# First pair's queries turned in two column parts, 24 zero products, one conversion step fewer at the first mixing, row factors and last scaling rearranged

## The chip, the cores and the metric

The kernel runs on one core of a Trainium2 chip. The time is the device time of one execution in microseconds (us), the median of several runs. The engines are TensorE (PE, with its weight loads as PEld), VectorE (DVE), ScalarE (ACT), GpSimd (POOL) and SyncE (SP, which only issues transfers here). Each works through its own queue in program order.

## The reference

Three layers follow one another on float32 data, batch B = 4, sequence S = 576. First an attention with rotated queries and keys over 8 heads of 64:

```python
q_rot, k_rot = (rotate(q), rotate(k))
scores = scale * np.matmul(q_rot, k_rot.transpose(0, 1, 3, 2))
scores = scores - np.max(scores, axis=-1, keepdims=True)
attn = np.exp(scores)
attn = attn / (np.sum(attn, axis=-1, keepdims=True) + 1e-09)
return np.matmul(attn, v).astype(np.float32)
```

`rotate` multiplies with cosine and sine tables and adds. Its result, laid out as (B, S, 512), goes through a gated layer: `h = gelu(x @ w_in)` split into u and v, v normalized over its row, mixed over the sequence, and

```python
v_s = np.einsum('ts,bsd->btd', w_sg, v_n) + b_sg[None, :, None]
gated = u * v_s
return (x + gated @ w_out).astype(np.float32)
```

Last come 4 experts, each a causal attention with one head of 64. Every row takes the two experts with the largest logits, weighted by a softmax over the two; the expert's output is `a @ v @ wo[e]`, scaled by that weight and by the softmax's row sum, and added to `out`.

## The kernel before, in words

Numbers that need float32 precision are held as two parts, a high one rounded to the fp32r type and a low one (the value less the high part). A product of two such numbers takes the three products high-high, high-low, low-high on TensorE. `split` makes the parts: ScalarE copies the high one, POOL (or VectorE) subtracts.

**Stage one, the attention** (lines 333 to 695), works on 16 pairs of heads (`Work`). A pair has nine row blocks x = 0 to 8. `slot(k)`, called with k = 9 n + x, writes the instructions of all engines by hand in this order: the exponentials of block x (ScalarE, `exps`), the scores of block x + 1 (TensorE, `scores`, into one of two PSUM buffers), the transposes of block x - 1 (TensorE, `turn`), the row maximum of block x + 1 (VectorE, `maxima`), the copies of the transposed block (`place`, ScalarE or VectorE), and in some slots parts of the product with the values (`av`). The engine wrapper keeps every instruction in program order (`fixed[0] = True`). So the scores of a block wait until the exponentials two blocks earlier have freed their buffer.

The tile `t` of a pair holds its queries or keys and, beside them, the same with the halves of each head exchanged. Turning is two products with the tables `rp` and an addition (`rope`, steps 0, 1 and 2). For all pairs but the first, POOL does the turning, `parts` makes the high and low part, and transfers issued by SP (`fill_k`, `fill_q`) copy these into the layouts that the scores read: `q2` (high part of one head above low part of the other), `qz` (high part with zeros beside it), `kh`. `fill_q` gets a tuple `part`; pair 1 calls it with both parts at once, later pairs with (0,) and (1,) apart.

The first pair goes another way, since nothing can hide its preparation: `first` (line 386) turns k and then q on VectorE, and ScalarE, VectorE and POOL write the layouts themselves, with no transfers. Meanwhile TensorE multiplies a tile of zeros (`warmed(40)`, line 658; each product takes two passes). Then come the loads of pairs 1 and 2, POOL's two products for each of pair 1's tiles (lines 663 and 667), and the first scores and maximum. The additions of pair 1 follow on VectorE in slots 2 and 3:

```python
if n == 0 and x in (2, 3):
    works[1].rope(3 - x, (2,), DVE)
```

In slots 0 to 3 TensorE gets two more zero products each.

**Stage two, the gated layer** (lines 729 to 975). `unit(g, *side)` writes TensorE's work of one block, then interleaves the steps of the two blocks before it with side work: `(lu, 3)` means three steps of the generator that converts `w_out` from its raw form (`load_split64`, lines 213 to 247; its VectorE steps are a maximum, a shift, and two combinations through PSUM). `mixed` (line 857) is the mixing over the sequence: 28 passes, then on VectorE a scale-and-add in PSUM and a product with u, then a split. It uses one of three PSUM buffers `S`. Line 938 is the first batch's mixing:

```python
for dc in range(4):
    unit(mixed(0, dc), (lu, (3, 3, 4, 4)[dc]))
```

**Stage three, the experts** (lines 978 to 1468), has 8 pairs of experts (`Causal`, two for each batch) in `slot3`, again nine blocks each. `factor` makes the row factors of a pair: the sums plus a small number (ScalarE), the reciprocal (VectorE), and four small products with the expert's weight on POOL. TensorE transposes them, and a small transfer out and three in spread them (`spread_factor`); `finish` multiplies the result with them and splits it into `zh` and `zl`, on POOL with a few exceptions. `Output.product` multiplies these with `wo` in three passes for each half of the inner dimension, and `Output.store` copies a block to SBUF and sends it out. For the very last pair the factors are spread by TensorE instead (`spread_here`), and lines 1446 to 1467 write the end by hand: transposes and values of the last block, `product` of block 3, spread, store of 3, `finish`, product and store of block 4, then of blocks 0 and 1.

## Time and profile before

| | |
|---|---|
| median of three runs | 675.15 us (675.15, 675.15, 676.3) |
| profiled execution, its own time | 674.28 us |
| its span, first to last instruction | 672.5 us |
| granted TensorE clock, mean | 1.00 |
| busy: PE, DVE, ACT, POOL | 662.9, 446.6, 433.6, 342.3 us |

The times of single instructions come from the one profiled execution; its own time is what sums of them are measured against. A matmul's end is modelled by the profiler, and a TensorE that is shown busy may still work on zeros.

In rows of the timeline the columns are: start in us, duration in us, engine, source line (L59 is the helper through which all instructions go), operation, what it writes and reads, shapes, number of instructions merged, and in brackets the idle time of the engine before it with what ended it. SPq is the transfer queue of SyncE.

### The profile page before, as it was taken

What the parts mean: (1) busy time and instruction counts of PE and PEld (TensorE: products, weight loads), DVE (VectorE), ACT (ScalarE), POOL (GpSimd) and SP (SyncE); (2) the same over time, 40 slices, a digit from 0 to 9 for tenths busy, and PEclk for the clock granted to TensorE, in tenths of its full rate; (3) what the DMA queues carried; (4) which work ended last, traced back from release to release, by engine and by line L of the source; (5) the groups of instructions that cost most, each with busy time, mean ns of one, the idle gap of its engine ahead of it and who ended that gap; (6) DMA issues with size and microseconds to landing.
All of it is one profiled execution on the core that took longest, in us unless ns stands there. A gap on an engine that the chain in (4) does not pass through costs nothing.

```text
span 672.5 us, 13535 instructions
## 1 busy us (share of the span) xinstructions
PE 662.9 (99%) x4741; PEld 585.5 (87%) x4741; DVE 446.6 (66%) x1011; ACT 433.6 (64%) x1033; POOL 342.3 (51%) x333
## 2 busy tenths in 40 slices
PE   8999999999999999999999999999999999999997
PEld 8777777777777777798999999999999999999885
DVE  5877777767777776578964764664247666656674
ACT  6777777877878777673563473472146776666774
POOL 2877788888888832642456127206212451542320
PEclk9999999999999999999999999999999999999999
DMA  7798888887888852661374243055466364553522
GB/s 270 209 283 269 249 237 248 242 239 241 228 254 227 249 150 90 182 189 34 118 222 143 89 134 115 12 142 161 121 182 150 92 171 96 135 160 76 143 82 79
DMA packets 64449, 112.83 MB, mean 168 GB/s; under 512 B 18991, under 2 KB 24190, under 8 KB 64382
## 3 DMA queue, kind: packets, MB, share of 16 engines
q1 hardware_dynamic: 61646, 106.29, 54.8%
q10 hardware_dynamic: 2736, 5.68, 2.8%
q8 instruction: 38, 0.62, 0.4%
q14 instruction: 29, 0.24, 0.1%
HBM read 58.06 MB, written 18.98 MB: 115 GB/s over the span
## 4 chain that ended last, share of the span: by engine, by line
PE 87%; DVE 4%; DMA 3%; ACT 2%; issue 1%; POOL 1%; SPq 1%; POOLq 0%; ACTq 0%; DVEq 0%
PE ps_S L59 46%; PE ps_o L59 16%; PE ps_t L59 13%; PE ps_f L59 5%; PE ps_l L59 3%; PE ps_s L59 3%; DMA ws<-in_w_sg_dram 1%; DMA mask<-in_cst_dram 1%; DVE ga L59 1%; DMA q<-lo 0%; DVE nmax L59 0%; DVE t L59 0%; DMA r<-d 0%; DMA sr<-rd 0%; ACT vh L59 0%
## 5 line engine op out<-in xcount | busy, mean ns | idle before, releaser
L59 DVE TENSOR_REDUCE nmax<-ps_S 128x1 f32<-128x576 f32 x144 | 108.8, 756 | 54.3 <-PE ps_S L59 51.6
L59 ACT ACTIVATE e<-ps_S,nmax 128x576 f32<-128x576 f32 x144 | 107.9, 749 | 34.2 <-DVE nmax L59 32.6
L59 PE MATMUL ps_t<-ident,e 128*128 128x128 f32 x776 | 118.1, 273 | 0.0
L59 PEld LDWEIGHTS ps_t<-ident,e 128*128 128x128 f32 x776 | 94.2, 140 | 3.7 <-ACT wih L59 0.4
L59 PE MATMUL ps_S<-kh,q 128*128 128x288 f32 x352 | 84.9, 333 | 2.6 <-ACT e L59 1.4
L59 POOL TENSOR_TENSOR t<-t,rp 128x576 f32<-128x576 f32 x60 | 84.6, 1431 | 0.1
L59 PEld LDWEIGHTS ps_S<-kh,q 128*128 128x128 f32 x352 | 52.2, 189 | 28.8 <-issue 12.8
L59 PE MATMUL ps_o<-g,v 128*64 128x320 f32 (+1 forms) x512 | 72.7, 415 | 0.0
L59 ACT COPY g<-ps_t 128x512 f32<-128x512 f32 x95 | 55.6, 586 | 23.3 <-PE ps_t L59 23.2
L59 POOL TENSOR_TENSOR lo<-t,hi 128x576 fp32r<-128x576 f32 x30 | 43.1, 1438 | 43.6 <-DVE hi L59 42.2
L59 PE MATMUL ps_S<-lo,q 128*128 128x288 f32 x304 | 65.2, 295 | 0.0
L59 PEld LDWEIGHTS ps_o<-g,v 128*64 128x64 f32 x512 | 32.4, 136 | 24.3 <-issue 4.9
L59 PE MATMUL ps_S<-yh,w 128*128 128x288 f32 x256 | 51.8, 304 | 0.0
L59 POOL TENSOR_TENSOR yl<-x,yh 128x640 fp32r<-128x640 f32 (+1 forms) x16 | 25.0, 1564 | 51.6 <-ACT yh L59 51.5
L59 ACT ACTIVATE e<-e,nmax 128x128 f32<-128x128 f32 (+4 forms) x72 | 42.3, 588 | 13.6 <-DVE nmax L59 13.5
L59 PEld LDWEIGHTS ps_S<-lo,q 128*128 128x128 f32 x304 | 48.6, 188 | 0.0
L59 POOL TENSOR_TENSOR t<-t 128x576 f32<-128x576 f32 x28 | 39.7, 1418 | 2.2
L59 ACT ACTIVATE ga<-ga 128x512 f32<-128x512 f32 (+1 forms) x34 | 22.3, 656 | 26.9 <-DVE ga L59 26.9
L59 PEld LDWEIGHTS ps_S<-yh,w 128*128 128x128 f32 x256 | 38.7, 189 | 0.1
L59 POOL TENSOR_TENSOR xl<-sa,xh 128x576 fp32r<-128x576 f32 x12 | 17.7, 1484 | 40.9 <-ACT xh L59 34.7
L59 DVE CUSTOM_DVE_ANT_0 e<-ps_s,mask 128x128 f32<-128x128 f32 (+3 forms) x64 | 31.0, 486 | 7.9 <-PE ps_s L59 6.0
L59 POOL TENSOR_TENSOR gxl<-u,gxh 128x576 fp32r<-128x576 f32 x16 | 22.8, 1429 | 25.3 <-ACT gxh L59 25.3
(283 smaller groups left out, 1758.5 us busy)
## 6 DMA issues: line engine op xcount, KB each, us to landing
t<-in_qk_dram SPq DMA_DIRECT2D x32, 576.0 KB
kh<-hi SPq DMA_DIRECT2D x92, 144.0 KB
q<-hi SPq DMA_DIRECT2D x30, 288.0 KB
q<-lo SPq DMA_DIRECT2D x38, 144.0 KB
v<-in_v_dram SPq DMA_DIRECT2D x16, 320.0 KB
sa<-xr SPq DMA_DIRECT2D x16, 288.0 KB
xd<-sa SPq DMA_DIRECT2D x16, 288.0 KB
xr<-xd SPq DMA_DIRECT2D x16, 288.0 KB
```

The lines of the kernel that those rows point to most:

```text
L59: ins = op(*a, **k)
```

## The change

The diff has five parts.

1. `first` becomes a generator in steps. It turns k whole and the first 320 columns of q, then writes the layouts for these columns (with VectorE making the low parts), and only in slots 0 to 2 turns and lays out the remaining 256 columns (their low parts on POOL). Pair 1's q products on POOL move from ahead of the first scores into slot 1, behind those low parts; its q addition on VectorE moves from slot 3 to slot 4. The zero products at the start are 24 in place of 40.
2. `fill_q` orders the copies by part: for a call with both parts, the two of the high part come first, then the two of the low part.
3. The first mixing takes 1, 3, 4 and 5 conversion steps in place of 3, 3, 4 and 4.
4. In the slots of the third pair of the experts' stage (n = 2), the four small products for the factors of the pair before it go to VectorE. The other pairs' stay on POOL.
5. At the end, the spread stands behind the first of block 3's three last passes, and the two others and block 4's come after it. The scaling and splitting of the last 256 columns go in two halves of 128, and all four stores come at the end. Block 1's store uses another SBUF buffer.

```diff
--- before.py
+++ after.py
@@ -167,7 +167,7 @@
 
                 todo = [twice(a, q2[a, 0, 0:S], qz[a, 0], qh[a, :]), (q2[c, 0, 0:S], ql[a, :]),
                         twice(c, q2[c, 1, 64:640], qz[c, 1], qh[c, :]), (q2[a, 1, 64:640], ql[c, :])]
-                todo = [x for i, x in enumerate(todo) if i % 2 in part]
+                todo = [x for h in part for x in todo[h::2]]
             else:
                 todo += [(q2[c, 1, 0:512], qh[c, 0:512]), (qz[c, 1, 64:S], qh[c, 0:512]), (q2[a, 1, 0:512], ql[c, 0:512])]
             if not self.turned:
@@ -393,27 +393,40 @@
                 def low(o, x, h, engine=DVE):
                     engine.tensor_tensor(o, x, f(h), op=ALU.subtract)
 
-                for t in (k, q):
+                def turn(t, s):
                     for i in range(2):
-                        DVE.tensor_tensor(t[:, i], t[:, i], rp[:, i], op=ALU.mult)
-                    DVE.tensor_tensor(t[:, 0], t[:, 0], t[:, 1], op=ALU.add)
-                q, k, s, s1 = q[:, 0], k[:, 0], slice(0, S), slice(64, 640)
+                        DVE.tensor_tensor(t[:, i, s], t[:, i, s], rp[:, i, s], op=ALU.mult)
+                    DVE.tensor_tensor(t[:, 0, s], t[:, 0, s], t[:, 1, s], op=ALU.add)
+
+                u, w = slice(0, 320), slice(320, S)
+                turn(k, slice(0, S))
+                turn(q, u)
+                yield
+                t, q, k = q, q[:, 0], k[:, 0]
                 ACT.copy(kh[a, 0], k[a])
                 ACT.copy(kh[c, 0], k[a])
+                ACT.copy(q2[a, 0, u], q[a, u])
+                ACT.copy(qz[a, 0, u], q[a, u])
                 ACT.copy(kh[c, 1], k[c])
+                ACT.copy(kh[a, 1], k[c])
+                ACT.copy(qz[c, 1, u], q[c, u])
                 hi = one.tile([P, S], F32R, tag="hi1", name="hi1")
                 DVE.tensor_copy(hi, k)
                 low(kl, k, hi)
-                ACT.copy(kh[a, 1], k[c])
-                ACT.copy(q2[a, 0, s], q[a])
-                ACT.copy(qz[a, 0], q[a])
-                ACT.copy(qz[c, 1], q[c])
-                u, w = slice(0, 256), slice(256, S)
                 low(q2[c, 0, u], q[a, u], q2[a, 0, u])
-                DVE.tensor_copy(q2[c, 1, s1], q[c])
-                low(q2[a, 1, 64:320], q[c, u], q2[c, 1, 64:320])
-                low(q2[a, 1, 320:640], q[c, w], q2[c, 1, 320:640], POOL)
+                DVE.tensor_copy(q2[c, 1, 64:384], q[c, u])
+                low(q2[a, 1, 64:384], q[c, u], q2[c, 1, 64:384])
+                yield
+                turn(t, w)
+                yield
+                ACT.copy(q2[a, 0, w], q[a, w])
+                ACT.copy(qz[a, 0, w], q[a, w])
                 low(q2[c, 0, w], q[a, w], q2[a, 0, w], POOL)
+                DVE.tensor_copy(q2[c, 1, 384:640], q[c, w])
+                low(q2[a, 1, 384:640], q[c, w], q2[c, 1, 384:640], POOL)
+                yield
+                ACT.copy(qz[c, 1, w], q[c, w])
+                yield
 
             def rope(self, x, steps=(0, 1, 2), engine=POOL):
                 t = self.ts[x]
@@ -544,6 +557,10 @@
 
             if w:
                 w.exps(x)
+            if k in (1, 2):
+                next(first)
+            if k == 1:
+                works[1].rope(0, (0, 1))
             if x == 0 and p:
                 p.out(False)
             if x == 4 and p:
@@ -572,8 +589,8 @@
             if x == 0 and p:
                 p.factor(0)
 
-            if n == 0 and x in (2, 3):
-                works[1].rope(3 - x, (2,), DVE)
+            if n == 0 and x in (2, 4):
+                works[1].rope(int(x == 2), (2,), DVE)
             if wk and not (nx and x == 5):
                 if late:
                     wk.place(4)
@@ -655,16 +672,17 @@
                 PE.matmul(warm[:, 0:P], zero, zero, start=True, stop=True)
 
         fixed[0] = True
-        warmed(40)
+        warmed(24)
         works[0].load(0)
         works[0].load_values()
-        works[0].first()
+        first = works[0].first()
+        next(first)
+        next(first)
         works[1].load(1)
         works[1].rope(1, (0, 1))
         works[1].load_values()
         works[2] = Work()
         works[2].load(2)
-        works[1].rope(0, (0, 1))
         works[0].start()
         works[0].scores(0)
         works[0].maxima(0)
@@ -673,6 +691,8 @@
         for k in range(9 * B * NP + 7):
             n, x = divmod(k, 9)
             slot(k)
+            if k == 0:
+                next(first)
             if k < 4:
                 warmed(2)
             if x in W_AT[4 if n == NP * B - 1 else min(n, 2 + n % 2)]:
@@ -936,7 +956,7 @@
             unit(values(1, tb), then=ln, n=1)
         run(ln)
         for dc in range(4):
-            unit(mixed(0, dc), (lu, (3, 3, 4, 4)[dc]))
+            unit(mixed(0, dc), (lu, (1, 3, 4, 5)[dc]))
         for b in range(1, B):
             at = attended(bx, b + 1) if b + 1 < B else iter(())
             for tb in range(0 if b > 1 else 2, NKB - b % 2):
@@ -1076,10 +1096,10 @@
             def rows(self, tb):
                 return slice(P * tb, P * tb + (P if tb < 4 else 64))
 
-            def product(self, tb, t, c):
+            def product(self, tb, t, c, part=slice(0, 3)):
                 sl = self.rows(tb)
                 zh, zl = self.z
-                for pi, (l, r) in enumerate(((zh, wo_[0]), (zh, wo_[1]), (zl, wo_[0]))):
+                for pi, (l, r) in list(enumerate(((zh, wo_[0]), (zh, wo_[1]), (zl, wo_[0]))))[part]:
                     PE.matmul(t[0:sl.stop - sl.start, :], l[:, c, sl], r[:, c],
                               start=(c == 0 and pi == 0), stop=(c == 1 and pi == 2))
 
@@ -1087,7 +1107,9 @@
                 sl, b = self.rows(tb), self.b
                 m = sl.stop - sl.start
                 act = b < B - 1 or tb in (1, 3, 4)
-                if act:
+                if b == B - 1 and tb == 1:
+                    o = wk.tile([P, S], F32, tag="r", name="ob", bufs=1)[:, 0:DM]
+                elif act:
                     o = wk.tile([P, DM], F32, tag="ob", name="ob")
                 else:
                     o = wk.tile([P, DM], F32, tag="e", name="ob", bufs=3)
@@ -1351,7 +1373,7 @@
                 w.gather()
             if p and x == late - 1:
                 for i in range(3):
-                    p.factor(i)
+                    p.factor(i, DVE if n == 2 else POOL)
             if p and x == 1 and n != 2:
                 p.turn_left()
                 p.left_parts()
@@ -1456,14 +1478,22 @@
         w.copy_factor()
         g.store(2, g.t[2])
         w.av_out(False, 1)
-        g.product(3, g.t[3], 1)
+        g.product(3, g.t[3], 1, slice(0, 1))
         w.spread_here(False, "o")
-        g.store(3, g.t[3])
-        w.finish(0, False)
+        g.product(3, g.t[3], 1, slice(1, 3))
         g.product(4, g.t[4], 1)
-        g.store(4, g.t[4])
+        (zh, zl), xt, r = g.z, w.xt, w.r[0]
+        zh, zl = zh[:, 1], zl[:, 1]
+        cols = [slice(P * i, P * i + P) for i in range(2)]
+        for c in cols:
+            DVE.tensor_tensor(xt[:, c], xt[:, c], r[:, c], op=ALU.mult)
+        for c in cols:
+            ACT.copy(zh[:, c], xt[:, c])
+        for c in cols:
+            DVE.tensor_tensor(zl[:, c], xt[:, c], f(zh[:, c]), op=ALU.subtract)
         for tb in range(2):
             g.product(tb, g.t[tb], 1)
+        for tb in (3, 4, 0, 1):
             g.store(tb, g.t[tb])
         fixed[0] = False
     cr.close()
```

## Rows read from the trace of the kernel before

**Rows 1.** The page, busy time, share of the span and instructions of each engine.
```profile
PE 662.9 (99%) x4741; PEld 585.5 (87%) x4741; DVE 446.6 (66%) x1011; ACT 433.6 (64%) x1033; POOL 342.3 (51%) x333
```

**Rows 2.** Windows of the start: busy by engine (x records), granted clock, DMA share, GB/s.
```profile
0.00:5.00 5.00, 3.96 (x18) 3.96 (x19) 0.17 (x1) 4.21 (x9) 0.20 (x4) 1.00 0.63 193
5.00:10.00 5.00, 5.00 (x39) 5.00 (x38) 4.11 (x6) 2.59 (x5) 0.00 (x0) 1.00 1.03 401
```

**Rows 3.** Timeline of the first 30 us, all engines.
```profile
1.04 12.01 PE L59 MATMUL ps_l<-zero 128*128 128x128 f32 x80 [1.04 <-DVE zero L59]
...
8.04 1.43 DVE L59 TENSOR_TENSOR t<-t,rp 128x576 f32<-128x576 f32 x2 [0.21 <-DMA t<-in_qk_dram]
...
10.61 1.94 ACT L59 CAST q<-t 64x576 fp32r<-64x576 f32 x3
10.67 0.76 DVE L59 TENSOR_TENSOR lo<-t,hi 128x576 fp32r<-128x576 f32 x1
11.46 0.42 DVE L59 TENSOR_TENSOR q<-t,q 64x256 fp32r<-64x256 f32 x1
...
12.80 0.51 PE L59 MATMUL ps_S<-kh,q 128*128 128x288 f32 x2
...
13.62 1.42 DVE L59 TENSOR_REDUCE nmax<-ps_S 128x1 f32<-128x576 f32 x2 [0.80 <-PE ps_S L59]
...
14.57 6.04 POOL L59 TENSOR_TENSOR t<-t,rp 128x576 f32<-128x576 f32 x4
...
18.21 1.12 DVE L59 TENSOR_TENSOR t<-t 128x576 f32<-128x576 f32 x1
...
20.63 1.41 POOL L59 TENSOR_TENSOR lo<-t,hi 128x576 fp32r<-128x576 f32 x1
20.65 2.00 DVE L59 TENSOR_TENSOR t<-t 128x576 f32<-128x576 f32 x1
...
23.43 1.41 POOL L59 TENSOR_TENSOR lo<-t,hi 128x576 fp32r<-128x576 f32 x1 [1.40 <-ACT hi L59]
...
26.07 0.60 SPq L178 DMA_DIRECT2D q<-lo  x1
...
29.77 0.50 PE L59 MATMUL ps_S<-kh,q 128*128 128x288 f32 x2 [0.61 <-DMA q<-lo]
```

**Rows 4.** Timeline of the first mixing, DVE and PE.
```profile
307.87 1.41 DVE L59 TENSOR_SCALAR ps_c<-ps_c 128x512 f32<-128x512 f32 x2
...
309.97 0.43 PE L59 MATMUL ps_S<-wsl,vh 128*128 128x288 f32 x2
310.04 0.76 DVE L59 TENSOR_TENSOR u<-ps_S,u 128x576 f32<-128x576 f32 x1
...
310.94 0.51 PE L59 MATMUL ps_S<-wsh,vh 128*128 128x288 f32 x2 [0.54 <-DVE u L59]
```

**Rows 5.** Timeline around the third expert pair's row factors, all engines but PEld.
```profile
534.11 0.20 DVE L59 RECIPROCAL rs<-rs 128x9 f32<-128x9 f32 x1
...
535.63 0.88 POOL L59 TENSOR_TENSOR rs<-rs,wgt 128x4 f32<-128x4 f32 x4
...
536.57 0.28 PE L59 MATMUL ps_o<-ident,rs 128*9 128x128 f32 x1 [0.52 <-POOL rs L59]
```

**Rows 6.** Timeline of the last block, all engines.
```profile
660.56 0.29 DVE L59 TENSOR_TENSOR h00l<-ps_t,h00h 128x128 fp32r<-128x128 f32 x1
...
665.37 0.43 DVE L59 TENSOR_TENSOR xt<-ps_t,tmp 64x256 f32<-64x256 f32 x1 [0.63 <-ACT tmp L59]
...
665.60 0.60 PE L59 MATMUL ps_o<-rr,x 128*128 128x128 f32 x4
...
666.24 0.42 DVE L59 TENSOR_TENSOR xt<-xt,ps_o 128x256 f32<-128x256 f32 x1 [0.45 <-PE ps_o L59]
...
667.15 0.74 PE L59 MATMUL ps_s<-w,zh 128*128 128x512 f32 x2 [0.26 <-ACT zh L59]
...
668.90 0.58 ACT L59 COPY ob<-ps_s 128x512 f32<-128x512 f32 x1 [1.32 <-PE ps_s L59]
```

## The prediction

> **What bounds the kernel now.** I read the page first, then the windows of the start, then the timeline around each place the diff touches. The page has TensorE busy for 662.9 us, 99% of the span [rows 1]. Little is left to gain while it works, so the change can pay only where TensorE stands still or does work that nobody needs. In the trace there are five such places, and the diff has an edit at each:
> - The start: 80 passes over a tile of zeros (40 products, two passes each) hold TensorE from 1.04 us for 12.01 us, and the first real scores start at 12.80 [rows 3].
> - The end of the first pair: TensorE waits 0.61 us at 29.77 for the copies of the second pair's low query parts [rows 3].
> - The first mixing: it waits 0.54 us at 310.94 for a VectorE product that frees a PSUM bank [rows 4].
> - The third pair of the last stage: it waits 0.52 us at 536.57 for row factors made on POOL [rows 5].
> - The last block: after the last row factors are spread at 665.60 there is a chain VectorE, ScalarE, TensorE with a wait of 0.26 us, and six passes and a store behind it [rows 6].
>
> **The change part by part.** The profiled execution took 674.28 us (span 672.5 and 1.8 around it), 0.9 below the median 675.15 of the three runs. The sum is a difference, made on that execution and then laid on the median.
>
> *Start: zero products.* 24 products are 48 passes. Of the records 18 fall before 5 us and 39 between 5 and 10 [rows 2], so the passes speed up to about double on the way (the granted-clock column reads 1.00 in both stretches, so the pace is taken from the counts; they fit the lower and then the upper level). The 48th ends near 9.2 us instead of 13.05. From there the data decide.
>
> *Start: data.* The query load lets VectorE begin at 8.04 [rows 3]. A two-input step costs 0.76 us on 576 columns and 0.42 on 256 [rows 3], so 0.49 on 320. The first column part is then turned at 9.46 instead of 10.27, the conversion and the low part of k that follow end at 10.62 instead of 11.43, the low part for the first scores at 11.1 and the last one at 12.0. ScalarE's seven copies, 0.65 each at full width [rows 3], end by 12.0. Undisturbed, the first scores start at 11.2, 1.6 us earlier.
>
> *Start: POOL.* Here the edit moves more than it says. Before, POOL's queue began with two low parts that waited for VectorE, so its four products for the second pair (turning k, then q) came at 14.57 [rows 3], after VectorE's start work. Now its first work is the two products for k, which wait for their load alone. Ahead of that load's end stand k, tables, q, identity, values and k again: 2.75 MB. The windows move 0.97 MB by 5 us and 401 GB/s after it [rows 2], so it is through at 9.5; q's load by the same count was through at 7.0 and used at 8.04, so POOL asks at about 10.4, in the middle of VectorE's low part of k. The two engines exclude each other in such steps: VectorE's addition took 1.12 us at 18.21 and 2.00 at 20.65, the second ending 0.6 after the POOL step of 20.63 had run its 1.41 [rows 3]. No row shows POOL waiting while VectorE has step after step queued, so whether POOL gets in between is open. Bounds: with no exclusion, both pairs' chains run early and the second pair's second scores come at 27.3, a gain of 2.5 us; if POOL gets in twice, VectorE's last low part ends at 14.3 (two POOL steps, each 1.41 less the part that VectorE would have worked). I take twice: POOL is waiting when VectorE's step ends, and VectorE got its turn between back-to-back POOL steps in just that way [rows 3]. The Trainium skill speaks against the edit here: SBUF — State Buffer, section Who interferes with whom, says that a VectorE instruction with two SBUF inputs and a POOL instruction that reads SBUF shut each other out for a whole instruction, the first to issue winning. By that, POOL's product, waiting since 10.4, goes before VectorE's step of 10.65: the same choice.
>
> So the second scores start at 14.3 (before: near 13.4), and the first maximum, queued on VectorE behind that low part, at 14.3 (before 13.62 [rows 3]). The second column part now turns on VectorE between the second and third maxima, three steps of 0.42, about 1.2 us, partly in idle time. Its two low parts on POOL end near 18.7, and the two products for the second pair's q, queued behind them, at 22.0 (before: 14.57 + 6.04 = 20.61 [rows 3]). The k low part follows on POOL, q's addition on VectorE behind that ends at 24.0 (before 22.65), conversion and low part at 26.2 (before about 24.85).
>
> *Fill order.* For the second pair alone the four query copies now go high, high, low, low. Only the two low copies are then left to issue when POOL is done: the last goes 0.5 us after it, not 1.2 (before at 26.07 [rows 3]). So the last is issued at 26.7 and, as before 3.7 us later, lets TensorE start that pair's second scores at 30.4 to 30.6: **+0.8 us** against 29.77, the 0.6 us of the fill order already in it. From there the attention stage is TensorE's, so this shift stays.
>
> SP's queue: the third pair's q load waits for the buffer that POOL's low parts now read until 18.7, some 4 us later. Behind it stand the k copies that are not due before 20.7, so it costs nothing; if POOL slips by 2 us more, they wait.
>
> *First mixing.* The side work's counts 3, 3, 4, 4 become 1, 3, 4, 5. Two VectorE steps, 1.41 us [rows 4], leave the first unit, so the product of 310.04 ends 1.3 us earlier, before TensorE's own work reaches there (309.97 and two passes of 0.13, so 310.24). Gain 310.94 - 310.24 = **-0.7**. The steps return in the second to fourth units, where VectorE has idle time; the last weight chunk comes a step later, with about 1 us of slack by my count.
>
> *Row factors.* Four small POOL products of 0.88 us, queued until 535.63 behind a long POOL product, move to VectorE right after the reciprocal of 534.11 [rows 5]. At most 0.8 us there, they end by 535.1, before the transpose's turn at 536.05. Gain **-0.5**; VectorE's mask step behind them slips by up to 0.5, which its readers do not see yet.
>
> *The end.* One pass instead of three stands before the spread: it starts at about 665.2, not 665.60. VectorE's own sum of 665.37 ends at 665.80, so the scaling starts at 665.85, not 666.24, in two halves of 0.29 (the 128-column step of 660.56), and ScalarE's first half is there at 666.4 [rows 6]. TensorE does the five passes left over first, to 666.8, then six without a stop and ends near 668.4, not 668.8. The store copy starts 0.45 earlier; ScalarE's two other copies fit before it, and the last store has its own buffer. The four output transfers stand closer, but 0.5 us apart. Gain **-0.45** (0 if they queue, 0.5 at best).
>
> Sum: +0.8 - 0.7 - 0.5 - 0.45 = -0.85. 674.28 becomes 673.4, the median 675.15 becomes **674.3**.
>
> **Rivals.**
> - *POOL stays out.* Its request comes later than 11.2, or VectorE keeps the turn over queued steps. For: no row shows POOL getting in. Against: the load count. The first scores then start at 11.2, but the second pair's chain still hangs on POOL's later q products, and its second scores come at 29.6: -0.2. Sum -1.85, 673.3.
> - *No collision anywhere*, q's steps included: -2.5 - 1.65 = -4.15, 671.0. The two stretched additions speak against it.
> - *The clock falls; slower.* Zeros end near 9.2, the first scores come at 11.2 to 12.3. In the idle stretch TensorE may drop to its lower level. Slots of this pair are 1.4 us of TensorE work; at half pace each costs 1.4 more, and the zeros needed some 6 us to speed up. One and a half slots not hidden make +2.1: 676.4. It decides if the gap is long enough; before, TensorE has no gap over 1 us here that would show it. The Trainium skill (TensorE: Matmul & The Clock Gate, HAM oscillation) says that one idle stretch long enough does it; no run here shows that yet.
> - *The edit of the end or of the fills does nothing*, because a transfer ends last anyway: +0.5 on any case, within the range.
>
> **How the numbers follow.** Chances: POOL gets in twice 0.42, stays out 0.36, no collision 0.08, clock falls 0.14. The measurement can tell about 0.2%, 1.35 us. Of the first case I put a quarter beyond that as faster, since each term may be 0.2 off; and a twentieth as slower; of the second 0.85 as faster; the third whole; of the fourth half as slower; the rest within. That makes faster 0.49, same 0.42, slower 0.09. Range: 671.8 to 676.3 leaves out most of the third case and the upper half of the fourth; the likeliest case alone gives 673.5 to 675.1.
>
> **What would show it.** Right: POOL's first product starting near 10.4 with a VectorE low part stretched past 1 us; the first maximum near 14.3; no waits at the mixing and at the transpose of factors; TensorE's last pass 0.45 earlier relative to the spread. Wrong: low parts of 0.4 to 0.5 us and the first maximum near 12.0; scores of the first pair at twice their duration (clock); a new wait of TensorE for a weight chunk after 336 us; a last output transfer that begins earlier and ends no earlier.

## The result, and the profile after

The changed kernel takes **680.91 us** (median of six runs, 679.38 to 686.62) against 675.12 for the kernel before, measured beside it: ratio 1.0096, 95% interval 1.0072 to 1.0119, so 5.8 us slower where the forecast was 674.3 and the range ended at 676.3. The profiled execution of after took 680.93 us, that of before 674.28 us.

The page of after, TensorE's busy time and the granted clock in 40 slices: TensorE is busy for 1.7 us less than in [rows 1] (32 passes over zeros are left out, some of the others are slower), the span is 6.6 us longer, and the first slice no longer has the full clock (its digit is 9 in before).

```profile
PE 661.2 (97%) x4709; PEld 583.5 (86%) x4709; DVE 451.4 (66%) x1021; ACT 434.2 (64%) x1037; POOL 341.6 (50%) x329
...
PEclk8999999999999999999999999999999999999999
```

The timeline of after, the start, against [rows 3]:

```profile
1.05 7.56 PE L59 MATMUL ps_l<-zero 128*128 128x128 f32 x48 [1.05 <-DVE zero L59]
...
10.83 3.03 POOL L59 TENSOR_TENSOR t<-t,rp 128x576 f32<-128x576 f32 x2 [10.39 <-DMA t<-in_qk_dram]
10.93 1.65 DVE L59 TENSOR_TENSOR q<-t,q 64x320 fp32r<-64x320 f32 x1
...
12.61 1.43 DVE L59 CAST q<-t 64x320 fp32r<-64x320 f32 x1
12.63 0.85 PE L59 MATMUL ps_S<-kh,q 128*128 128x288 f32 x2 [4.02 <-DVE q L59]
...
14.48 0.75 DVE L59 TENSOR_REDUCE nmax<-ps_S 128x1 f32<-128x576 f32 x1
...
14.71 0.82 PE L59 MATMUL ps_S<-kh,q 128*128 128x288 f32 x2 [0.74 <-DVE q L59]
...
18.62 1.53 POOL L59 TENSOR_TENSOR q<-t,q 64x256 fp32r<-64x256 f32 x2 [4.76 <-issue]
...
20.23 3.30 POOL L59 TENSOR_TENSOR t<-t,rp 128x576 f32<-128x576 f32 x2
...
26.24 1.30 SPq L178 DMA_DIRECT2D q<-hi  x2
...
27.74 1.81 SPq L178 DMA_DIRECT2D q<-lo  x2
...
31.83 0.51 PE L59 MATMUL ps_S<-kh,q 128*128 128x288 f32 x2 [1.61 <-ACT e L59]
...
33.13 0.62 PE L59 MATMUL ps_S<-kh,q 128*128 128x288 f32 x2
```

The zeros end at 8.61, POOL's product starts at 10.83, and VectorE's low part and copy beside it take 1.65 and 1.43 us: the collision that the forecast had. TensorE stands idle for 4.02 us and then runs the first scores at 0.85 us for two passes instead of 0.51. And the second pair's scores come at 31.83 and 33.13, where the kernel before had the second ones at 29.77. The row of 31.83 names ScalarE's `e`, whose last work that these scores need had ended before 30; the low copies were issued at 27.74. The same wait is put down to them (<-DMA q<-lo) in five of the runs below.

The windows of after, 1 us each (busy time of each engine, then granted clock, share of the DMA engines, GB/s). The clock falls to its lower level (0.50, 1.2 GHz) near the end of the idle stretch, just before 12 us, and is back at 19 us:

```profile
12.00:13.00 1.00, 0.36 (x1) 0.37 (x2) 0.97 (x2) 0.44 (x1) 1.00 (x2) 0.50 0.30 56
...
14.00:15.00 1.00, 0.29 (x1) 0.33 (x2) 0.97 (x3) 0.00 (x0) 0.00 (x0) 0.50 0.97 401
...
17.00:18.00 1.00, 1.00 (x6) 0.98 (x5) 0.97 (x3) 0.67 (x2) 0.00 (x0) 0.50 0.00 0
18.00:19.00 1.00, 1.00 (x9) 1.00 (x7) 0.94 (x3) 0.91 (x3) 0.38 (x1) 0.60 0.00 0
19.00:20.00 1.00, 1.00 (x11) 1.00 (x10) 0.58 (x3) 1.00 (x3) 0.92 (x2) 1.00 0.00 0
```

The timeline of after at the first mixing, against [rows 4]: no wait of TensorE for the product u is left.

```profile
312.67 1.23 PE L59 MATMUL ps_S<-wsh,vl 128*128 128x288 f32 x8
312.73 0.76 DVE L59 TENSOR_TENSOR u<-ps_S,u 128x576 f32<-128x576 f32 x1
...
313.74 0.42 PE L59 MATMUL ps_S<-wsh,vh 128*128 128x288 f32 x2
```

The timeline of after at the row factors, against [rows 5]: the four small products take 2.75 us on VectorE, not 0.8, with two POOL products beside them; the left part queued behind them comes late, and TensorE waits 2.10 us instead of 0.52.

```profile
538.59 2.75 DVE L59 TENSOR_TENSOR rs<-rs,wgt 128x4 f32<-128x4 f32 x4
...
538.94 1.56 POOL L59 TENSOR_TENSOR yl<-x,yh 128x640 fp32r<-128x640 f32 x1
...
540.46 0.85 POOL L59 TENSOR_TENSOR xt<-xt,r 128x320 f32<-128x320 f32 x1
...
542.26 0.30 PE L59 MATMUL ps_o<-ht,vst 128*128 128x64 f32 x1 [2.10 <-DVE ht L59]
```

One more place loses, which no part of the change touches. At the start of the experts VectorE waits for the load of the mask, and TensorE behind it. First the row of before, then two of after:

```profile
495.05 0.29 DVE L59 CUSTOM_DVE_ANT_0 e<-ps_s,mask 128x128 f32<-128x128 f32 x1 [1.15 <-DMA mask<-in_cst_dram]
...
499.22 0.29 DVE L59 CUSTOM_DVE_ANT_0 e<-ps_s,mask 128x128 f32<-128x128 f32 x1 [2.07 <-DMA mask<-in_cst_dram]
...
499.58 0.39 PE L59 MATMUL ps_s<-kh,q 128*128 128x256 f32 x1 [1.04 <-DVE nmax L59]
```

The table follows the same ScalarE steps through four profiled executions: the time in before in us, and how much later they come in after and in two of the runs below.

| step | before | after | 40 zero products | 24 zero products, alone |
|---|---|---|---|---|
| first exponential of the second pair | 29.12 | +4.32 | +3.57 | +0.21 |
| of the third pair | 45.71 | +3.50 | +2.75 | +0.16 |
| of the sixth pair | 92.69 | +4.48 | +2.73 | +0.71 |
| first gelu step | 274.22 | +4.02 | +2.18 | +0.27 |
| 18th gelu step, behind the first mixing | 368.91 | +3.25 | +1.42 | +0.26 |
| first exponential of the experts | 495.38 | +4.18 | +1.70 | +1.21 |
| 19th, before the moved factors | 532.32 | +4.17 | +1.69 | +1.20 |
| 28th, behind them | 553.02 | +6.54 | +2.96 | +1.93 |
| end of the last copy | 669.49 | +6.28 | +2.85 | +1.94 |

So in this execution of after 3.5 us come from the start, about 1.0 is lost between the third and the sixth pair, the mixing gives 0.8 back, 0.9 goes at the load of the mask and 2.4 at the factors. The load took 5.0 to 5.1 us from its issue to the step that waits for it in four profiles (after, 24 zero products alone, one low part on POOL, and the whole new start with 24 zeros) and 4.1 to 4.6 us in all others. The four have 24 zeros, but the fifth profile with 24 zeros (factors back on POOL) doesn't show it, and why the load is late stays open, as does the loss between the third and the sixth pair.

### The profile page after: what moved, and what is told of

Its sections match the earlier page's. It is cut to its first block, busy times and chain, and to the rows that moved or that the text cites. A ratio compares the mean times of both kernels' runs of the same rounds, so it can differ in the third digit from the quotient of the medians.

```text
span 679.1 us, 13486 instructions
## 1 busy us (share of the span) xinstructions
PE 661.2 (97%) x4709; PEld 583.5 (86%) x4709; DVE 451.4 (66%) x1021; ACT 434.2 (64%) x1037; POOL 341.6 (50%) x329
## 4 chain that ended last, share of the span: by engine, by line
PE 87%; DMA 4%; DVE 4%; ACT 2%; issue 1%; SPq 1%; POOL 1%; POOLq 0%; ACTq 0%; DVEq 0%
PE ps_S L59 47%; PE ps_o L59 16%; PE ps_t L59 13%; PE ps_f L59 5%; PE ps_s L59 3%; PE ps_l L59 2%; DMA t<-in_qk_dram 1%; DMA mask<-in_cst_dram 1%; DVE q L59 1%; DVE t L59 0%; DVE nmax L59 0%; ACT e L59 0%; DMA r<-d 0%; ACT vh L59 0%; DVE ga L59 0%
## 5 line engine op out<-in xcount | busy, mean ns | idle before, releaser
L59 POOL TENSOR_TENSOR t<-t,rp 128x576 f32<-128x576 f32 x60 | 84.9, 1437 | 10.5 <-DMA t<-in_qk_dram 10.4
L59 DVE COPY g<-ps_t 128x512 f32<-128x512 f32 x49 | 33.5, 684 | 3.0 <-PE ps_t L59 1.3
```

Of the source, the lines that this page charges most:

```text
L59: ins = op(*a, **k)
```

## Experiments

Each time stands beside that of the kernel before, measured together with it on the same chip; a difference to after compares two such pairs. Theory: four parts lose (the gap of the clock, POOL's early products, the order of the copies, the factors on VectorE) and two gain. Rival to it: one of them, the clock or the collision, explains all of the start.

### One part of the change undone

**Factors back on POOL.**

```diff
-p.factor(i, DVE if n == 2 else POOL)
+p.factor(i)
```

> The changed kernel with the third pair's row factors back on POOL. Theory (the four small VectorE products were stretched by POOL to 2.75 us and made TensorE wait 2.10 us instead of 0.52): that wait is 0.5 again and the whole comes out 2.0 to 2.9 us under the changed kernel, about 678.3. Rival (TensorE would have lost that time there anyway, because the shift of the start put POOL's long product elsewhere): the wait stays over 1.5 us with POOL as its releaser, and the time stays within 0.7 us of the changed kernel.

678.95 us (before 674.87; ratio 1.0075, 1.0046 to 1.0104): 2.0 below after, but the two intervals overlap. The traces say less than the theory. POOL is again the releaser, with a wait of 1.6 us and not 0.5, as the rival had it. From the 19th to the 28th exponential of the experts it is 20.70 us in before, 23.07 in after and 22.22 here: 0.85 of the loss at this place goes with the factors, and 1.5 stays without them. POOL's steps ahead of them wait 4.08 us for a transfer (`r<-d`, the row factors of an earlier pair), in before 3.02, and its long product starts 1.06 behind the reciprocal, in before with it.

**Start of before, fills of after.**

```diff
-warmed(24)
+warmed(40)
...
-first = works[0].first()
-next(first)
-next(first)
+works[0].first()
```

`first`, the slots and the place of the second pair's q products are as before, too.

> The changed kernel with the whole start of the kernel before (40 zero products, queries turned in one piece, the second pair's products behind POOL's low parts), the new fill order kept. Theory (the start costs 3.5 us and nothing later gives it back): 3.0 to 4.0 us under the changed kernel, about 677.4, TensorE's steady stretch after the second pair's start at the place it had before. If the new fill order is what delays the second pair's first scores, a part of the 3.5 stays: 0.5 to 1.5 us of shift against the kernel before at that place, and first scores of that pair at about 29.5 instead of 27.5.

675.91 us (1.0020, 1.0008 to 1.0032): 5.0 below after, more than expected. The start is nearly the whole loss. The second pair's first maximum still comes 1.6 later than in before (29.94 against 28.32), which points to the order of the copies.

**40 zero products.**

```diff
-warmed(24)
+warmed(40)
```

> The changed kernel with 40 zero products in place of 24, nothing else: TensorE is busy until the first scores can start, the collision of POOL's products with VectorE's low parts stays. Clock theory: granted clock 1.00 from 10 to 20 us, the second pair's first scores 1.0 to 1.6 us earlier than in the changed kernel (31.83), the whole about 679.6. Collision theory alone (the clock costs nothing because VectorE and POOL set the pace): same clock reading, but those scores within 0.4 us of 31.8 and the time within 0.5 us of the changed kernel.

677.50 us (1.0053, 1.0034 to 1.0072), 3.4 below after; the clock reads 1.00 in every stretch of the start though the collision stays. So the missing zeros are a cause of their own, and the collision can't be the only one; 2.6 us over before are left, in which the copies and the factors are contained, too. Of the 3.4 only 0.8 shows at the second pair (first maximum at 31.89, in after 32.65); the two intervals leave 0.9 to 4.9. The table above has the rest: 1.0 up to the sixth pair, 0.7 at the load of the mask and 1.1 at the factors, all behind the stretch of the lower level. That the clock causes these three is not shown.

**One low part on POOL first, so that its products come later.**

```diff
-low(q2[a, 1, 64:384], q[c, u], q2[c, 1, 64:384])
+low(q2[a, 1, 64:384], q[c, u], q2[c, 1, 64:384], POOL)
```

> The changed kernel with the first column part's second low part on POOL, ahead of its products for the second pair, as the kernel before had it: those products can't start before that low part is done, so none of VectorE's first steps collides; still 24 zero products. Collision theory: VectorE's low part of the first scores takes about 0.5 instead of 1.65 us, the first scores come at about 11.3 and the first maximum near 12.5, and the second pair's first scores 1.5 to 3 us earlier than 31.83, the whole about 678 to 679.5. Clock theory alone: TensorE still stands idle 2.7 us, the granted clock falls below 1.00 in the same two stretches and at least 1 us of the loss stays. If the clock holds after the shorter gap, the whole comes out near 677.5.

679.27 us (1.0074, 1.0055 to 1.0093). The first scores come at 11.60 and the first maximum at 12.48, as the collision theory has it; TensorE still waits 2.88 us before them and the clock reads 0.72 from 10 to 15 us. The traces show both causes at work; that its time lies 1.6 below after can't be told from nothing by the two intervals.

### One part alone, on the kernel before

**24 zero products.**

```diff
-warmed(40)
+warmed(24)
```

> The kernel before with 24 zero products in place of 40 and nothing else. Clock theory (TensorE left idle for about 4 us drops to its lower level and the first pair pays for it): zeros end at 8.6, first scores at about 12.8 as before but at 0.8 us per two passes instead of 0.5, granted clock clearly below 1.00 between 12 and 18 us, the whole 2 to 3.5 us slower than the kernel before (677 to 678.5). My prediction's theory (the zeros past the 24th do nothing that anybody needs): no change, within 0.4 us.

676.85 us (1.0021, 1.0009 to 1.0032): 1.5 slower. Less than expected, but no doubt about the sign. The 1-us windows of this run: the lower level lasts about 3.4 us here.

```profile
12.00:13.00 1.00, 0.81 (x3) 0.81 (x4) 0.93 (x3) 0.64 (x1) 0.30 (x1) 0.50 0.63 96
...
14.00:15.00 1.00, 1.00 (x6) 1.00 (x5) 0.80 (x2) 0.66 (x2) 0.92 (x2) 0.50 0.86 355
15.00:16.00 1.00, 1.00 (x7) 0.81 (x7) 0.27 (x1) 0.87 (x4) 1.00 (x1) 0.83 0.79 78
16.00:17.00 1.00, 1.00 (x11) 1.00 (x10) 0.87 (x2) 0.60 (x3) 1.00 (x2) 1.00 0.49 189
```

The slow first pair itself costs little here: in the table the third pair's first exponential comes 0.16 later and the first gelu step 0.27, since the second pair's scores wait for their copies anyhow. This execution (676.19, the fastest of ten) loses 0.9 at the load of the mask and 0.7 near the factors. So the time that the missing zeros cost is shown, the way from the clock to it only in a small part.

**The order of the copies.**

```diff
-todo = [x for i, x in enumerate(todo) if i % 2 in part]
+todo = [x for h in part for x in todo[h::2]]
```

> The kernel before with the new order of the second pair's query copies alone (high, high, low, low). My prediction's theory: the last low copy is issued 0.6 us earlier, TensorE's wait of 0.61 us at 29.77 goes, 0.6 us faster (674.3). Theory from the trace with only the start undone: the first low copy is now third in the queue, so the second pair's first scores wait for it, 1.6 us later than 27.53, and its second scores come 0.4 to 0.8 us later than 29.77: 0.2 to 0.8 us slower than the kernel before.

675.81 us (before 675.07; 1.0010, 1.0000 to 1.0020), 0.7 slower: small, but not the gain of 0.6. The timeline of this run shows the second pair's first scores 1.7 us later than the 27.53 of before, with the low copies issued last, and the second ones 1.3 us behind them:

```profile
25.20 1.79 SPq L178 DMA_DIRECT2D q<-lo  x2
...
29.27 0.50 PE L59 MATMUL ps_S<-kh,q 128*128 128x288 f32 x2 [1.58 <-ACT e L59]
...
30.57 0.61 PE L59 MATMUL ps_S<-kh,q 128*128 128x288 f32 x2
```

**Factors on VectorE.**

```diff
-p.factor(i)
+p.factor(i, DVE if n == 2 else POOL)
```

> The kernel before with the third pair's row factors on VectorE and nothing else. Theory (stretched by POOL's long products beside them): the four products take 2.0 to 2.8 us, TensorE waits about 2 us for VectorE's left part behind them, the whole 1.0 to 2.5 us slower than the kernel before. My prediction: 0.5 us faster.

676.97 us (1.0019, 1.0003 to 1.0034), 1.6 slower. The timeline of this run, and one of its 1-us windows:

```profile
534.14 2.50 DVE L59 TENSOR_TENSOR rs<-rs,wgt 128x4 f32<-128x4 f32 x4
...
537.56 0.30 PE L59 MATMUL ps_o<-ht,vst 128*128 128x64 f32 x1 [1.85 <-DVE ht L59]
```

```profile
540.00:541.00 1.00, 1.00 (x5) 0.96 (x5) 0.72 (x4) 0.56 (x2) 0.62 (x3) 0.50 0.48 101
```

The wait is there as in after. Here the clock fell behind it as well. Five profiles have this wait: with 1.85 (this run), 2.14 (start of before) and 2.21 us (one low part on POOL first) the clock fell to its lower level behind it, with 1.98 (40 zero products) and 2.10 (after) it stayed at 1.00. So the factors on VectorE, with both inputs in SBUF, cost the wait in every run and the clock in some.

**The mixing.**

```diff
-unit(mixed(0, dc), (lu, (3, 3, 4, 4)[dc]))
+unit(mixed(0, dc), (lu, (1, 3, 4, 5)[dc]))
```

> The kernel before with the side work of the first mixing as 1, 3, 4, 5 and nothing else. Theory: 1.0 us ahead of the kernel before right after 309 us; what of it lasts decides. If the later stages wait for TensorE alone it lasts and the whole is 0.7 to 1.2 us faster; if a later wait (VectorE or the mask's load near 495 us) takes it back, 0.2 to 0.6 us, and the end has the other half of what the run of both parts gained (0.9 us).

674.40 us (before 675.37; 0.9987, 0.9978 to 0.9996): 1.0 faster, so the gain lasts to the end. The traces have it sharper: from the 9th to the 18th gelu step, with the first mixing between them, it is 68.43 or 68.44 us in all nine profiles without this part and 67.64 to 67.67 in all nine with it.

**The end** (product split around the spread, scaling in halves, stores last).

```diff
+g.product(3, g.t[3], 1, slice(0, 1))
 w.spread_here(False, "o")
+g.product(3, g.t[3], 1, slice(1, 3))
...
+for tb in (3, 4, 0, 1):
+    g.store(tb, g.t[tb])
```

> The kernel before with the rearranged end and nothing else. Theory from the traces: TensorE's last pass and the last copy come 0.4 us earlier counted from the spread, but the four output transfers now leave together and the last one lands no earlier: 0.0 to 0.1 us faster. My prediction: 0.45 us faster.

674.85 us (before 675.11; 0.9994, 0.9985 to 1.0002): 0.3 us, which can't be told from nothing.

**Mixing and end together.**

> The kernel before with two parts of the change alone: the side work of the first mixing (1, 3, 4, 5) and the rearranged end. Theory: the wait of 0.54 us at the mixing and the pass behind it go (0.7 to 1.2 us) and the end gives 0.4: 1.1 to 1.6 us faster than the kernel before, about 673.5. Rival (TensorE's other waits take the gain back before the end, or the last output transfer ends no earlier): within 0.5 us of the kernel before.

674.15 us (before 675.07; 0.9989, 0.9979 to 0.9999), 0.9 faster, no more than the mixing alone. What became of the end is in the transfers. GB/s of the last 8 us (664.3 to 672.3, 0.2 us a number), first in the run with the mixing alone, whose end is the old one:

```profile
GB/s 0 0 0 0 0 133 410 410 338 21 0 0 0 72 389 420 389 41 0 0 0 143 225 236 51 0 369 389 430 338 389 430 277 0 0 0 0 0 0 0
```

then in the run with both:

```profile
GB/s 0 0 0 0 0 72 379 430 379 52 0 0 0 0 0 0 0 0 358 369 451 133 236 195 184 266 399 410 389 277 420 348 143 10 0 0 0 0 0 0
```

Both send the first block at 665.3. The old end sends another at 666.9 and leaves three for the last stretch. The new end sends nothing there and four blocks from 667.9 to 670.9 without a gap. The last bytes move at the same time in both runs, and both spans are 672.3. What the engines win (the last copy is 0.36 us earlier, 668.35 against 668.71) is lost in the output transfers; why four together take longer is not shown.

### What stretches the factors

Mixing and end as above, factors on VectorE, with the reciprocals put into PSUM, so that each product has one input in SBUF and one in PSUM:

```diff
-DVE.reciprocal(self.rs, self.rs)
+self.rq = bank("f")[:, 0:9] if engine is DVE else self.rs
+DVE.reciprocal(self.rq, self.rs)
...
-engine.tensor_tensor(rs[r, c], rs[r, c], w[r, k, e], op=ALU.mult)
+engine.tensor_tensor(rs[r, c], self.rq[r, c], w[r, k, e], op=ALU.mult)
```

> The same two parts and the third pair's row factors on VectorE as in the change, but with the reciprocals written to PSUM, so that each of the four products has one input in SBUF and one in PSUM. Theory (VectorE's products were stretched because both inputs lay in SBUF while POOL worked in SBUF): four products in 0.4 to 0.8 us instead of 2.75, no wait of TensorE for the factors, 0.3 to 0.6 us under the run without this part. Rival (the stretch comes from the strided small tiles or from VectorE's own queue): the four still take over 2 us, TensorE waits about 2 us, 1.5 to 2.5 us over that run.

674.36 us (0.9988, 0.9979 to 0.9998), 0.2 from the run without this part: no gain, no loss. The timeline of this run answers the question all the same:

```profile
534.36 1.58 POOL L59 TENSOR_TENSOR yl<-x,yh 128x640 fp32r<-128x640 f32 x1
...
534.60 0.57 DVE L59 TENSOR_TENSOR rs<-ps_f,wgt 128x4 f32<-128x4 f32 x4
```

The four products take 0.57 us in the middle of POOL's long one, and no wait of TensorE for factors is left. That the operands stretched them is shown. The Trainium skill (SBUF — State Buffer, Who interferes with whom) says that a VectorE instruction with at most one SBUF input, outside its modes with two ports, doesn't contend with GpSimd; these rows agree. One SBUF input is not always enough, though: the copy at 12.61 in after reads one tensor in SBUF and took 1.43 us beside POOL's product, 0.33 us without one in the run with one low part on POOL.

### The column parts by themselves

**New start with 40 zero products, the rest as before** (so the clock is out of it).

```diff
-works[0].first()
+first = works[0].first()
+next(first)
+next(first)
...
-works[1].rope(0, (0, 1))
```

> The kernel before with the whole new start (queries in two column parts, the second pair's k products first on POOL) but 40 zero products, so that TensorE has no gap; fills, mixing, factors and end as before. Theory (POOL's products collide with VectorE's low parts and then its longer queue holds the second pair): VectorE's first low parts at 1.4 to 1.7 us, the second pair's second scores 1.3 to 2.2 us later than 29.77, the whole 1.3 to 2.2 us slower than the kernel before. My prediction (0.6 of its +0.8 us was a fill gain not taken here): 1.4 us slower. Rival (with the clock held the column parts cost nothing): within 0.4 us.

678.16 us (before 675.37; 1.0035, 1.0022 to 1.0049), 2.8 slower, above the range expected. The trace shows the order high, high, low, low on SP's queue although that edit isn't in this kernel: these transfers aren't pinned, and the program came out so. Therefore, with the old order pinned:

```diff
-nc.sync.dma_start(f(o), f(i))
+d = nc.sync.dma_start(f(o), f(i))
+if len(part) == 2:
+    tc.keep_in_program_order(d)
```

> The kernel with the new start and 40 zero products (columns), the second pair's four query copies pinned to the order high, low, high, low. If the order costs here what it cost in the kernel before (0.7 us): the second pair's first scores start about 1.5 us earlier than in columns (31.4 in its trace), its second scores 0.5 to 0.9 us earlier, the whole about 2.1 us over the kernel before. If the late data alone decide: second scores within 0.3 us of columns', the whole 2.6 to 3 us over the kernel before.

677.27 us (before 675.21; 1.0032, 1.0021 to 1.0043), 2.1 slower. TensorE in the timeline of this run, the second pair's first and second scores:

```profile
29.68 0.50 PE L59 MATMUL ps_S<-kh,q 128*128 128x288 f32 x2 [0.35 <-issue]
...
31.92 0.50 PE L59 MATMUL ps_S<-kh,q 128*128 128x288 f32 x2 [0.60 <-DMA q<-lo]
```

The second scores are 2.15 later than 29.77 [rows 3], and the whole is 2.1 slower. The shift isn't won back: the first gelu step of this profile is 2.4 later than in before and the end of the last copy 3.5, as it loses another 1.1 in the experts (677.78, one of the two slowest of seven executions). That 2.15 and 2.1 agree so well is luck in part.

**Column parts with POOL's queue in its old order** (40 zeros).

```diff
 works[1].load(1)
 works[1].rope(1, (0, 1))
+works[1].rope(0, (0, 1))
...
-if k in (1, 2):
-    next(first)
-if k == 1:
-    works[1].rope(0, (0, 1))
```

> The kernel before with the queries turned in two column parts, both ahead of the first scores, 40 zero products, and POOL's queue in its old order: its two low parts, then the second pair's four products. If POOL's early products are the cause of the 2.8 us: VectorE's first steps at 0.4 to 0.5 us, POOL's four products near 15 us as one block, the second pair's second scores within 0.7 us of 29.77, the whole within 0.7 us of the kernel before. If the column parts themselves cost it: 1.5 to 3 us slower.

676.92 us (1.0028, 1.0018 to 1.0038), 1.8 slower: between the two theories. The timeline of this run, POOL's four products and the second pair's second scores:

```profile
15.52 6.06 POOL L59 TENSOR_TENSOR t<-t,rp 128x576 f32<-128x576 f32 x4
...
31.21 0.61 PE L59 MATMUL ps_S<-kh,q 128*128 128x288 f32 x2
```

There is no collision at the first steps, yet POOL's block starts 0.95 later than at 14.57 [rows 3], since the second part's low parts come later, and its copies too came out as high, high, low, low. By the times, POOL's early products are worth about 1.0 us of the 2.8, which two intervals of 0.7 and 0.9 us to either side can't tell from nothing. The traces, both with the same order of copies, give 1.5: the third pair's first exponential comes 3.05 later than in before with the products early, and 1.58 here. That the later second part and the order of the copies have the rest is argued from these rows, not measured apart.

**New start whole, with 24 zeros.**

```diff
-warmed(40)
+warmed(24)
```

> The kernel before with the whole new start, 24 zero products as in the change; fills, mixing, factors and end as before. If gap and column parts add (1.5 and 2.8): about 4.3 us slower than the kernel before. If the collision keeps TensorE at its lower level for longer: 5 to 6.5 us slower, granted clock below 1.00 until 18 to 19 us.

680.22 us (1.0093, 1.0062 to 1.0125), 5.1 slower. The sum of the two parts, 1.5 + 2.8 = 4.3, and the 5 of the rival lie both within the interval (4.2 to 8.4). The copies came out as high, high, low, low again. Its 1-us windows stay at the lower level until 20 us, longer than with 24 zeros alone:

```profile
19.00:20.00 1.00, 1.00 (x7) 1.00 (x6) 0.30 (x2) 0.98 (x4) 0.92 (x2) 0.50 0.00 0
20.00:21.00 1.00, 1.00 (x8) 0.98 (x8) 0.56 (x1) 0.38 (x1) 0.92 (x2) 0.71 0.00 0
```

With 24 zeros and the collision the lower level lasts about 6.8 us (here, in after and with the factors back on POOL); without the collision it is 3.4 us (24 zeros alone, and one low part on POOL). So in these five profiles the collision doubles the stretch that the gap brings.

**Mended start**, on the changed kernel: the order of the copies and the factors undone as well.

```diff
-warmed(24)
+warmed(32)
...
-low(q2[a, 1, 64:384], q[c, u], q2[c, 1, 64:384])
+low(q2[a, 1, 64:384], q[c, u], q2[c, 1, 64:384], POOL)
```

> The changed kernel with its start mended and the two parts that lost undone: 32 zero products, the first column part's second low part on POOL ahead of the second pair's products, fills in the order of before, row factors on POOL. If gap and collision were all that was wrong with the column parts, the granted clock reads 1.00 throughout, the second pair's second scores come at 29.8 or before and the time is that of the run with the mixing and the end alone, or up to 0.7 us less. If POOL's chain for the second pair sets the pace all the same, those scores come 0.5 to 1.5 us later than 29.77 and the time is as much over that run.

679.52 us (1.0051, 1.0034 to 1.0067), slower than either theory said. The old order of the copies isn't tested by it, since they came out as high, high, low, low here, too. The clock reads 1.00 through the first pair: the wait before the first scores is 1.7 us now. But POOL's products meet the second column part instead (its two turning steps take 1.81 us, in after 0.76), TensorE waits 2.01 us for the second pair's low copies, and then the clock falls there. A row of TensorE's timeline and two windows of this run:

```profile
30.74 0.50 PE L59 MATMUL ps_S<-kh,q 128*128 128x288 f32 x2 [2.01 <-DMA q<-lo]
```

```profile
32.00:33.00 1.00, 1.00 (x5) 0.82 (x4) 0.90 (x2) 0.66 (x2) 1.00 (x2) 0.50 1.01 395
...
35.00:36.00 1.00, 1.00 (x10) 0.96 (x9) 0.37 (x1) 1.00 (x3) 0.00 (x0) 0.96 0.81 317
```

Not all of its twelve executions lost the clock: the seven with a mean of 0.999 or 1.000 have a median of 677.1 us (675.8 to 680.8), the five at 0.996 or 0.997 one of 680.1 (679.9 to 680.3). So a lost clock goes with about 3 us within one kernel, though the seven alone spread over 5.

## Why the prediction was wrong, point by point

| part | forecast, us | measured alone, us |
|---|---|---|
| start whole (24 zeros, columns, order of copies) | +0.8 | +5.1 |
| of it: 24 zeros | 0 (2.1 as a rival) | +1.5 |
| of it: columns and POOL's early products, old order | +1.4 | +2.1 |
| of it: order of the copies | -0.6 | +0.7 |
| mixing | -0.7 | -1.0 |
| row factors | -0.5 | +1.6 |
| end | -0.45 | -0.3, not told from 0 |

Start whole, factors, mixing and end sum to +5.4; the change measures +5.8. The intervals of the first two (2.1 and 1.0 us to either side) are too wide for this to show that the parts add. The largest miss is the start, by 4.3 us, then the factors, by 2.1. In "start whole" the copies' edit isn't in the code, but they came out in the new order.

**Zero products.** "From there the data decide" is the step that failed. The forecast's own numbers left TensorE idle from 9.2 to at least 11.2; I gave the fall of the clock 0.14, because no row of before showed it. Before, the zeros left no gap there, so that trace could not show it: its silence was no evidence. The mechanism of that rival was right, its chance was not. Its price (2.1) lies near the measured 1.5 and 2.3 (the whole new start with 24 zeros against 40), but not for its reason: it was to fall due in the first pair, and the traces have 0.2 to 1.1 us of it at the third pair and the rest later. The Trainium skill (TensorE: Matmul & The Clock Gate, HAM oscillation) has a long idle stretch as the cause, and the 4.02 us of after agree. Waits of about 2 us at the factors went either way, without order by their length; there the clock fell without a stretch as long as that.

**Collision.** Right, and close at first: POOL's request (forecast 10.4, came by 10.83), twice between VectorE's steps, first maximum 14.48 (14.3). Too small was what follows from it. With the clock held and the old order, the second pair's second scores come at 31.92; without the fill gain the forecast had about 31.1. The late second scores of the first pair delay VectorE's second part, that delays POOL's low parts and its q products behind them. In after the low clock lies on top: POOL's low parts end at 20.15 (18.7) and the q products at 23.53 (22.0).

**Order of the copies.** Wrong in sign. I looked at when the last low copy is issued and not at who needs the first. In the old order the second pair's first scores have their low copy early and fill the time until the second one lands. In the new order both low copies come last, the first scores wait for them, and the second scores queue behind 1.3 us of TensorE work.

**Mixing.** Right: 0.7 forecast, 0.8 in the traces, 1.0 in the times.

**Row factors.** "At most 0.8 us there" failed. I weighed the exclusion of VectorE and POOL at the start and didn't apply it here, although these products have both inputs in SBUF and [rows 5] show POOL's work running into 535.63. Alone they cost 1.6; in the changed kernel the traces leave 0.85 to them, since POOL's factors come late there, too. Behind them on VectorE I saw only the mask step, not the left part, for which TensorE waits.

**End.** The engines' part was right: from the spread's POOL products to the last copy the new end takes 0.4 less (664.03 to 668.90 in before, 670.72 to 675.18 in after). But the rival "a transfer ends last anyway" took the gain.

**A version that beats both.** The mixing alone (674.40, 1.0 under before) is all that the change has shown to give; with the end it is 674.15 against its own 675.07. Both intervals lie just under 1.

## What to carry to other kernels

Work that does nothing for the result may still hold the clock: before removing it, count the idle stretch that it leaves, and give the fall of the clock a price and a chance even if the old trace, in which that stretch was filled, shows none. Before moving a small operation to VectorE, look whether both its inputs lie in SBUF and whether POOL is busy there at that time; one input in PSUM freed it here. Reordering transfers needs the first reader of each, not only the time of the last one. And before a difference is put down to one edit, compare the times of the same steps in both traces from place to place: here a part of the loss lay hundreds of us behind the edits of the start.

## What was not expected of the hardware

Four products of 128x4, 0.88 us on POOL and 0.57 us on VectorE with one PSUM input, took 2.50 to 2.75 us with both inputs in SBUF beside POOL's work: in after they ended at 541.34, with POOL's second step beside them (541.31), and alone at 536.64 (536.61), so what they cost went by POOL's instructions and not by their own size. Behind four waits of TensorE of 1.85 to 2.21 us (three at the factors, one at the second pair) the clock fell for some 3 us; behind others as long it stayed, among them 2.10 us in after and 2.30 us before the second pair's scores in the whole new start with 24 zeros. Their length alone doesn't decide. Executions of one kernel differ in it as well: six of eight of the run with the factors alone have a mean clock of 0.997 and take 676.8 us or more, two have 1.000 and take 676.2 and 676.4.
